# Half of q's norm on ScalarE, fused additions on GpSimd, later stores and loads: one change to a tuned attention + MLP kernel

## The chip, the cores and the metric

One core of one Trainium2 chip. The metric is the device time of one execution in microseconds (us). "Start" and "end" times inside a profile count from the start of its span. In this kernel TensorE does the matrix products (busy 1379.2 of 1399.7 us before the change) into PSUM, in banks that the program names; VectorE, ScalarE and GpSimd work beside it (busy 802.2, 419.6 and 581.7 us). The granted clock is the share of its full clock that the profile shows for TensorE.

## The reference, cut

```python
# q, k, v: (8, 12, 448, 64) f32;  w_in: (768, 2048), w_out: (2048, 768) f32
def rmsnorm(x, g):
    return x / np.sqrt(np.mean(x * x, axis=-1, keepdims=True) + 1e-06) * g
q_n, k_n = rmsnorm(q, g_q), rmsnorm(k, g_k)
attn = softmax(q_n @ k_n.T / sqrt(64))            # per batch and head
x = (attn @ v) -> (8*448, 12*64)                  # heads side by side
out = relu(x @ w_in) ** 2 @ w_out                 # (3584, 768)
```

The heads are handled two at a time: 48 pairs. The first twelve pairs (i = 0 to 11) run alone, and beside them GpSimd prepares the weights: each product of the MLP is done with seven block products instead of eight (Strassen's way), which needs sums of weight blocks (S1 to S4). The other pairs run beside the second product. The change touches the first twelve pairs, 0 to about 135 us, and the start of the first product after it.

## The kernel before: the parts concerned

```python
# weights: four ticks a tile t (generator; a tick after each part of an attention iteration)
    n = t - 3
    if there(n) and n % 2:                                  # tick 1: store of a finished pair of tiles, 1.3 MB
        nc.sync.dma_start(dst, blocks_of(n)[:, 0:7]); written[0] = n + 1
    nc.vector.tensor_scalar(e, e, ..., ALU.max, ALU.min)
    yield                                                   # tick 2: ScalarE and VectorE (cut)
    yield                                                   # tick 3
    nc.vector.scalar_tensor_tensor(eu, high, 0xC0000000, bits, ...)
    total(t - 2, S3, A11, A21, ALU.subtract)                # total: one GpSimd addition of 128x384
    total(t - 2, S4, A12, S2, ALU.subtract)
    value(t - 1, 0)                                         # value: one GpSimd addition of 128x384
    yield                                                   # tick 4
    value(t - 1, 1)
    total(t - 1, S1, A21, A22, ALU.add)
    total(t - 1, S2, S1, A11, ALU.subtract)
    load_words(t, t - 1); yield
...
def norm(i):                                                # (cut)
    nc.scalar.activation(sq, raw, AF.Square)
    nc.vector.tensor_reduce(rstd, sq..., AX, ALU.add)
    nc.vector.tensor_scalar(rstd, rstd, 1.0 / D, 1e-6, ALU.mult, ALU.add)
    nc.gpsimd.tensor_tensor(flat, flat, mhalf, ALU.pow)     # rstd ** -0.5
    nc.gpsimd.tensor_tensor(sq[:, 0]..., raw[:, 0]..., rstd..., ALU.mult)   # q's norm, 112x512
...
def add_up(i, c):                                           # the "running sum" of the softmax
    nc.vector.tensor_tensor(acc, probs[i, 0] if c == 1 else acc, probs[i, c], ALU.add)   # 112x896
...
for i in range(NAT):                                        # attention_alone, one iteration (cut)
    if 0 < i < NAT - 3:
        load(i + 3)                                         # q and k of pair i+3
    scores(i, 0); scores(i, 1)                              # matmuls, then exponentials on ScalarE
    transpose(i + 1, 1, 0)                                  # k, PSUM bank 0, then a copy by ScalarE
    values(i - 1, (2, 3)); add_up(i, 1); norm(i + 2)
    yield
    transpose(i + 1, 0, 0)                                  # q, PSUM bank 0 as well
    load_v(i + 1); yield
    scores(i, 2); scores(i, 3); total_of(i - 1); values(i, (0, 1)); finish(i - 1); yield
    if added(i) == 3: add_up(i, 2)                          # odd iterations
    combine_x(i - 1); yield
values(i, (2, 3)); total_of(i); finish(i); combine_x(i)     # the last pair
```

All loads and stores shown go through one queue, that of SyncE (SP), in program order: a store that waits for GpSimd holds up every load behind it (until 74.88 us in the third reading below).

Of the kernel before, what the change touches and what calls it, by code (L numbers as in the profile page):

```python
# [9 lines left out]
F32 = mybir.dt.float32  # L10
U32 = mybir.dt.uint32
AF = mybir.ActivationFunctionType
# [291 lines left out]
def places_of(qk, i, work):  # L304


    first, second = i % 2 * 4 + work, i % 2 * 4 + 2 + (i // 2 + work) % 2
    return qk[:, first:second + 1:second - first]
# [78 lines left out]
def attention_then_ffn_bounded(  # L387
# [100 lines left out]


    A11, S2, S1, S3, A12, A22, S4 = range(7)  # L490
    A21 = 7
    w1s = dram.tile([HF, 7, P, HW], F32, name="w1s")
    w2s = dram.tile([7, HF // 4, P, 4, HW], F32, name="w2s")

# [4 lines left out]
    def words_of(n):  # L499
        place = n % WORDS  # L500
        if place == 0:
            at = BLOCKS * 8 * HW + EXPS * NW
            flat = stage[:, at:at + 2 * NW]
        elif place < 3:
            f = (NFC, HF)[place - 1] - 2
            flat = gT[:, f:f + 2, :].rearrange("p f n -> p (f n)")[:, 0:2 * NW]
        else:
            if (n, "words") not in spare:
                spare[n, "words"] = spare["pool"].tile([P, 2 * NW], F32, tag="words", name="words", bufs=WORDS - 3)
            flat = spare[n, "words"]  # L510
        return flat.bitcast(U32)

    def blocks_of(n):
        at = n // 2 % BLOCKS * 8 * HW
        return stage[:, at:at + 8 * HW].rearrange("p (k m) -> p k m", k=8)
# [27 lines left out]
    def prepare(t):  # L543



        def there(n):
            return 0 <= n < 2 * NFC

        def parts(n):  # L550
            low, high = pairs_of(words_of(n))
            return exponents_of(n), exponents_of(n).bitcast(U32), low, high

        def value(n, half):
            if not there(n):
                return

            to = ((A11, A12), (A21, A22)) if n < NFC else ((A11, A21), (A12, A22))
            dst = blocks_of(n)[:, to[n % 2][half]]
            part = slice(half * HW, (half + 1) * HW)  # L560
            if doubles:
                _, eu, low, _ = parts(n)
                nc.gpsimd.tensor_tensor(*[x.bitcast(I32) for x in (dst, low[:, part], eu[:, part])], ALU.add)  # L563
            else:
                nc.gpsimd.tensor_copy(dst, words_of(n).bitcast(F32)[:, part])

        def total(n, dst, x, y, op):
            if there(n) and n % 2:
                nc.gpsimd.tensor_tensor(*[blocks_of(n)[:, i] for i in (dst, x, y)], op)  # L569

        def unsigned(n):

            if there(n) and doubles:
                e, _, _, high = parts(n)
                nc.scalar.activation(e, high.bitcast(F32), AF.Abs)

        if t == 0:
            unsigned(0)
        n = t - 3
        if there(n) and n % 2:  # L580
            c = n % NFC // 2
            dst = w1s[c] if n < NFC else w2s[:, c // 4, :, c % 4]
            nc.sync.dma_start(dst.rearrange("k p m -> p k m"), blocks_of(n)[:, 0:7])
            written[0] = n + 1
        if there(t) and doubles:
            e, eu, low, high = parts(t)

            nc.vector.tensor_scalar(e, e, 2.0 ** -15, 1.875 * 2.0 ** 16, ALU.max, ALU.min)
        yield
        if there(t) and doubles:  # L590
            nc.scalar.activation(low.bitcast(I32), low, AF.Copy, scale=2.0 ** -29)
            bits = banks.get("bits", eu)
            nc.vector.tensor_scalar(bits, eu, 3, 0x3FFFFFF8, ALU.logical_shift_left, ALU.bitwise_and)
        if t < 3:
            load_words(t, t - 1)
        yield
        if there(t) and doubles:
            nc.vector.scalar_tensor_tensor(eu, high, 0xC0000000, bits, ALU.bitwise_and, ALU.bitwise_or)
        total(t - 2, S3, A11, A21, ALU.subtract)
        total(t - 2, S4, A12, S2, ALU.subtract)  # L600
        value(t - 1, 0)
        yield
        unsigned(t + 1)
        value(t - 1, 1)
        total(t - 1, S1, A21, A22, ALU.add)
        total(t - 1, S2, S1, A11, ALU.subtract)
        load_words(t, t - 1)
        yield

# [45 lines left out]
    def load(i):  # L655
        if i < NAT:
            load_q(nc, qk, q, i)
            load_k(nc, qk, k, i)
            return

        b, h0 = i // NPAIR, 2 * (i % NPAIR)
        for s, src in enumerate((q, k)):
            dst = by_squares(i, 0)[:, s]
            for n in range(4):
                nc.sync.dma_start(dst[n * 32:(n + 1) * 32],
                                  src[b, h0 + n // 2, :, n % 2 * 32:n % 2 * 32 + 32]
                                  .rearrange("(g t) e -> t g e", t=32))
# [16 lines left out]
    def norm(i):  # L684
        if i >= NAT:
            squares(i)
            return norm_by_squares(i)
        raw, sq = (places_of(qk, i, n)[:SP] for n in range(2))
        rstd = rstds[i] = small.tile([SP, 2, 2 * NJ], F32, tag="rstd", name="rstd", bufs=4)
        normed[i] = sq[:, 0], raw[:, 1]  # L690
        if i <= 2:
            return normalise_in_turn(nc, raw, sq, rstd, mhalf)
        nc.scalar.activation(sq, raw, AF.Square)
        nc.vector.tensor_reduce(rstd, sq.rearrange("p s (n d) -> p s n d", d=D), AX, ALU.add)
        nc.vector.tensor_scalar(rstd, rstd, 1.0 / D, 1e-6, ALU.mult, ALU.add)
        flat = rstd.rearrange("p s n -> p (s n)")
        nc.gpsimd.tensor_tensor(flat, flat, mhalf[:SP, 0:4 * NJ], ALU.pow)  # L697

        nc.gpsimd.tensor_tensor(sq[:, 0].rearrange("p (j h d) -> p h j d", j=NJ, h=2),  # L699
                                raw[:, 0].rearrange("p (h j d) -> p h j d", j=NJ, h=2),  # L700
                                rstd[:, 0].rearrange("p (h j) -> p h j ()", h=2).to_broadcast([SP, 2, NJ, D]),
                                ALU.mult)

    def squares(i):
        raw, qkn = (by_squares(i, n).rearrange("p s g e -> p (s g e)") for n in range(2))
# [27 lines left out]
    def transpose(i, s, n):  # L733

        pt = bank("pt", n)
        for j in range(NJ):
            nc.tensor.transpose(pt[:, j * SP:(j + 1) * SP], normed[i][s][:, j * P:(j + 1) * P], ident[:SP, :SP])  # L737
        if s:
            nc.scalar.copy(qkT[:, i % 2, s], pt)
        else:  # L740
            nc.scalar.activation(qkT[:, i % 2, s], pt, AF.Copy, scale=gains[:, 0:1])
# [58 lines left out]
    def values(i, chunks=range(NJ)):  # L800
        if 0 in chunks:
            pavs[i] = ps_o.tile([P, S], F32, tag="o", name="pav") if i >= NAT or i % 2 == 0 else bank("pav", 1)
        for c in chunks:
            for h in range(2):
                nc.tensor.matmul(pavs[i][h * D:(h + 1) * D, :], vs[i][:, h, c, :], probs[i, c][:, h, :],  # L805
                                 start=(c == 0), stop=(c == NJ - 1))
# [49 lines left out]
    def attention_alone():  # L856


        for i in range(NAT):
            more = i + 1 < NAT  # L860
            if 0 < i < NAT - 3:
                load(i + 3)
            scores(i, 0)
            scores(i, 1)
            if i == 0:

                transpose(1, 1, 1)
                scores(0, 2)
                scores(0, 3)
                transpose(1, 0, 0)  # L870
                add_up(0, 1)
                norm(2)
                load_v(1)
                values(0, (0, 1))
                load(3)
                yield
                continue
            if more:
                transpose(i + 1, 1, 0)
            values(i - 1, (2, 3))  # L880
            add_up(i, 1)
            if i + 2 < NAT:
                norm(i + 2)
            elif not more:
                norm(NAT)
                load(NAT + 2)
            yield
            if more:
                transpose(i + 1, 0, 0)
            load_v(i + 1)  # L890
            yield
            scores(i, 2)
            scores(i, 3)
            total_of(i - 1)
            values(i, (0, 1))
            finish(i - 1)
            yield
            if added(i) == 3:
                add_up(i, 2)
            combine_x(i - 1)  # L900
            if NAT <= i + 3 < NAT + 2:
                load(i + 3)
            yield
        values(i, (2, 3))
        total_of(i)
        finish(i)
        combine_x(i)

# [321 lines left out]
```

## Time and profile before

| | before |
|---|---|
| device time | 1400.38 us (3 runs, 1400.37 to 1401.83) |
| TensorE busy | 1379.2 of 1399.7 us |
| GpSimd / VectorE busy, 20 to 140 us | 106.2 / 105.1 of 120 us |
| first product starts | 134.21 us |

The prediction below shows the page and TensorE's waits. Groups of instructions further below, 20 to 140 us, are given as line, engine, operation, output and input, count, then busy us and mean ns of one, then the idle time before them with what ended it.

The timeline of VectorE and of GpSimd (start, length, engine, line, operation):

```profile
71.07 1.96 DVE L764 TENSOR_TENSOR gT<-gT 112x896 f32<-112x896 f32 x1
72.95 1.21 DVE L694 TENSOR_REDUCE rstd<-qk 112x16 f32<-112x1024 f32 x1
```

### The profile page before, as it was taken

The page shows a single profiled execution, that of the slowest core. Times are in us where ns is not written, and L with a number is a line of the kernel's source. Part 1 is how long each engine was busy: PE and PEld are TensorE (multiplying, and loading weights), DVE is VectorE, ACT ScalarE, POOL GpSimd, SP SyncE. Part 2 cuts the span into 40 slices and gives each one's busy share as a digit, 9 for nine tenths or more (in the row PEclk, how much of TensorE's full clock was granted, in tenths as well). Part 3 has the DMA queues.
Part 4 walks back from the last instruction along what each step waited for, and adds up shares of the span by engine and source line. Part 5 has one row for each costly group of instructions (what it writes and reads, how often), then busy time and mean ns, then how long its engine had stood idle before and what let it go on. Part 6 is the DMA issues. An engine that isn't in the chain of part 4 may idle for free.

```text
span 1399.7 us, 14445 instructions
## 1 busy us (share of the span) xinstructions
PE 1379.2 (99%) x4450; PEld 638.5 (46%) x4450; DVE 802.2 (57%) x1398; ACT 419.6 (30%) x621; POOL 581.7 (42%) x400
## 2 busy tenths in 40 slices
PE   8989999999999999999999999999999999999997
PEld 3333455444444454544444455444444445554553
DVE  6889676589876234476777523457777633332111
ACT  7875556432322011233332011233333201110000
POOL 5998877444552123544453122544445302221000
PEclk9999999999999999999999999999999999999999
DMA  9687998545764332344665333344564332334443
GB/s 240 189 229 199 341 384 306 143 97 120 144 121 105 102 90 85 104 113 110 127 130 119 97 94 90 98 106 105 129 126 102 95 101 85 90 87 104 106 111 70
DMA packets 430915, 188.79 MB, mean 135 GB/s; under 512 B 277484, under 2 KB 428780, under 8 KB 430828
## 3 DMA queue, kind: packets, MB, share of 16 engines
q1 hardware_dynamic: 421228, 179.05, 49.8%
q10 hardware_dynamic: 9472, 8.72, 2.3%
q8 instruction: 38, 0.62, 0.2%
q14 instruction: 49, 0.40, 0.1%
q0 software_dynamic: 128, 0.00, 0.0%
HBM read 154.54 MB, written 33.16 MB: 134 GB/s over the span
## 4 chain that ended last, share of the span: by engine, by line
PE 93%; POOL 3%; DVE 1%; DMA 1%; ACT 1%; issue 1%; ACTq 0%; POOLq 0%
PE ps L1047 37%; PE sc L749 10%; PE pd L1000 10%; PE pa L1000 10%; PE pc L1000 10%; PE pav L805 9%; PE pb L1000 5%; PE tot L819 1%; POOL rstd L697 1%; POOL gC L563 1%; DMA sw<-w1s 1%; POOL gC L569 1%; PE pt L737 0%; ACT gT L754 0%; POOL qk L699 0%
## 5 line engine op out<-in xcount | busy, mean ns | idle before, releaser
L1047 PE MATMUL ps<-gT,sw 128*128 128x448 f32 x768 | 299.2, 543 | 0.8 <-POOL gT L977 0.8
L719 POOL TENSOR_TENSOR half<-half,mhalf 128x28 f32<-128x28 f32 x36 | 173.6, 4822 | 266.9 <-DVE half L718 226.8
L1047 PE MATMUL ps<-gC,sw 128*128 128x448 f32 x576 | 225.2, 543 | 0.0
L977 POOL TENSOR_TENSOR gT<-gT 128x448 f32<-128x448 f32 x96 | 94.9, 990 | 309.9 <-ACT gT L973 309.9
L1047 PEld LDWEIGHTS ps<-gT,sw 128*128 128x128 f32 x768 | 144.1, 190 | 150.7 <-issue 147.0
L756 ACT ACTIVATE pr<-sc 112x896 f32<-112x896 f32 x120 | 104.7, 914 | 293.4 <-PE sc L749 184.9
L749 PE MATMUL sc<-qkT 64*112 64x448 f32 x768 | 170.6, 563 | 0.9 <-ACT qkT L383 0.8
L1047 PEld LDWEIGHTS ps<-gC,sw 128*128 128x128 f32 x576 | 108.2, 190 | 112.1 <-issue 110.8
L1000 PE MATMUL pa<-xT,sw 128*128 128x448 f32 x384 | 154.9, 540 | 0.0
L973 ACT ACTIVATE gT<-gT 128x448 f32<-128x448 f32 x96 | 55.3, 577 | 310.1 <-DVE gT L1015 310.0
L749 PEld LDWEIGHTS sc<-qkT 64*112 64x112 f32 x768 | 61.2, 173 | 97.9 <-issue 81.3
L1000 PEld LDWEIGHTS pa<-xT,sw 128*128 128x128 f32 x384 | 73.0, 190 | 71.6 <-issue 70.3
L805 PE MATMUL pav<-pr,vt 112*64 112x448 f32 x480 | 100.2, 547 | 0.0
L721 POOL TENSOR_TENSOR qk<-qk,half 128x448 f32<-128x448 f32 x72 | 81.3, 1150 | 2.8
L764 DVE TENSOR_TENSOR acc<-acc,pr 112x896 f32<-112x896 f32 x60 | 68.2, 1136 | 21.0 <-ACT pr L756 18.5
L1000 PE MATMUL pb<-xC,sw 128*128 128x448 f32 x192 | 77.6, 540 | 1.5 <-issue 1.5
L1000 PE MATMUL pd<-xT,sw 128*128 128x448 f32 x192 | 77.9, 542 | 0.0
L1000 PE MATMUL pc<-xC,sw 128*128 128x448 f32 x192 | 77.5, 540 | 0.2 <-DMA sw<-w1s 0.2
L1000 PE MATMUL pd<-xC,sw 128*128 128x448 f32 x192 | 77.5, 540 | 0.0
L1000 PE MATMUL pc<-xT,sw 128*128 128x448 f32 x192 | 77.4, 539 | 0.0
L1015 DVE TENSOR_TENSOR gT<-z,pd 128x448 f32<-128x448 f32 x32 | 19.8, 620 | 99.7 <-PE pd L1000 99.7
L569 POOL TENSOR_TENSOR gC<-gC 128x384 f32<-128x384 f32 x64 | 72.8, 1157 | 2.5
(120 smaller groups left out, 1551.0 us busy)
## 6 DMA issues: line engine op xcount, KB each, us to landing
sw<-w1s SPq DMA_DIRECT2D x224, 192.0 KB, 2.3
sw<-w2s SPq DMA_DIRECT2D x168, 256.0 KB, 3.3
w1s<-gC SPq DMA_DIRECT2D x8, 1344.0 KB, 7.5
w2s<-gC SPq DMA_DIRECT2D x8, 1344.0 KB, 7.6
out_dram<-osb SPq DMA_DIRECT2D x184, 56.0 KB, 1.9
qk<-in_q_dram SPq DMA_DIRECT2D x144, 56.0 KB, 3.0
qk<-in_k_dram SPq DMA_DIRECT2D x144, 56.0 KB, 2.9
vt<-in_v_dram SPq DMA_DIRECT2D x72, 112.0 KB, 2.9
```

Source lines behind the costliest of these rows:

```text
L569: nc.gpsimd.tensor_tensor(*[blocks_of(n)[:, i] for i in (dst, x, y)], op)
L719: nc.gpsimd.tensor_tensor(half, half, mhalf, ALU.pow)
L721: nc.gpsimd.tensor_tensor(qkn[:, s], raw[:, s], half[:, s * NG:(s + 1) * NG].rearrange("p g -> p g ()").to_broadcast([P, NG, 32]), ALU.mult)
L749: nc.tensor.matmul(sc[:, h, 0:S], qkT[rows, at, 1, c * SP:(c + 1) * SP], qkT[rows, at, 0, :], start=True, stop=True)
L756: nc.scalar.activation(pr, sc[:, :, 0:S], AF.Exp)
L764: nc.vector.tensor_tensor(acc, probs[i, 0] if c == 1 else acc, probs[i, c], ALU.add)
L805: nc.tensor.matmul(pavs[i][h * D:(h + 1) * D, :], vs[i][:, h, c, :], probs[i, c][:, h, :], start=(c == 0), stop=(c == NJ - 1))
L973: nc.scalar.activation(g, src, AF.Relu)
L977: nc.gpsimd.tensor_tensor(g, g, g, ALU.mult)
L1000: nc.tensor.matmul(ps, stream[n + i][:, c], rhs[:, c], start=first and c == 0, stop=c == HC - 1, skip_group_check=not first)
L1015: add(g, x, ps, ALU.add)
L1047: nc.tensor.matmul(ps, stream[n][:, c % 4], rhs_of[i][:, c], start=c == 0, stop=c == HF - 1)
```

## The change

Its intent is to take work from GpSimd, which limits the stage at 80 to 100 us (busy 19.5 of 20 us, TensorE 16.3): four small ScalarE operations do the first head of q's norm an iteration later, and additions on neighbouring blocks become one operation of 768 elements. ScalarE now reads q's buffer later, so the load of pair i+3 moves to the end of the iteration; the weight store moves two ticks down. Odd iterations use the other PSUM bank for q's transpose, and the end is reordered.

```diff
-    A21 = 7
+    A21 = -1
...  (store: from tick 1 to tick 3)
-        total(t - 2, S3, A11, A21, ALU.subtract)
-        total(t - 2, S4, A12, S2, ALU.subtract)
-        value(t - 1, 0)
+        total(t - 2, (S3, S4), (A11, A12), (A21, S2), ALU.subtract)     # one operation of 768
         yield
+        value(t - 1)                                                    # one operation of 768
         unsigned(t + 1)
-        value(t - 1, 1)
-        total(t - 1, S1, A21, A22, ALU.add)
-        total(t - 1, S2, S1, A11, ALU.subtract)
+        total(t - 1, (S1,), (A21,), (A22,), ALU.add)
+        total(t - 1, (S2,), (S1,), (A11,), ALU.subtract)
...  (norm: GpSimd multiplies only the second head, 112x256)
+    def norm_q(i):
+        if 2 < i < NAT:
+            dst, src, factors = q_of(i, 0)
+            for j in range(NJ):
+                nc.scalar.activation(dst[:, j], src[:, j], AF.Copy, scale=factors[:, j:j + 1])
...
-            if 0 < i < NAT - 3:
-                load(i + 3)
             scores(i, 0)
             scores(i, 1)
...
+            norm_q(i + 1)
             if more:
                 transpose(i + 1, 1, 0)
...
-                transpose(i + 1, 0, 0)
+                transpose(i + 1, 0, i % 2)
...
             finish(i - 1)
+            if i + 3 < NAT:
+                load(i + 3)
             yield
...
-        values(i, (2, 3))
+        values(i, (2,))
         total_of(i)
+        values(i, (3,))
```

More of the change, by code (lines that the diff above doesn't have):

```diff
@@ L552, in parts, with put, blocks, value @@
             return exponents_of(n), exponents_of(n).bitcast(U32), low, high
-        def value(n, half):
+        def put(op, *places):
+            lone = any(len(x) == 2 and x[1] <= x[0] for _, x in places)
+            for take in [slice(0, 1), slice(1, 2)] if lone else [slice(0, 2)]:
+                op(*[of[:, x[take][0]:x[take][-1] + 1:max(x[take][-1] - x[take][0], 1)] for of, x in places])
+        def blocks(n, *which):
+            return blocks_of(n), [1 + i for i in which]
+        def value(n):
             if not there(n):
@@ L558, in value, with add @@
             to = ((A11, A12), (A21, A22)) if n < NFC else ((A11, A21), (A12, A22))
-            dst = blocks_of(n)[:, to[n % 2][half]]
-            part = slice(half * HW, (half + 1) * HW)
+            halves = [x.rearrange("p (two m) -> p two m", two=2) for x in
+                      ((parts(n)[2], parts(n)[1]) if doubles else (words_of(n),))]
             if doubles:
-                _, eu, low, _ = parts(n)
-                nc.gpsimd.tensor_tensor(*[x.bitcast(I32) for x in (dst, low[:, part], eu[:, part])], ALU.add)
-            else:
-                nc.gpsimd.tensor_copy(dst, words_of(n).bitcast(F32)[:, part])
+                def add(*x):
+                    nc.gpsimd.tensor_tensor(*[y.bitcast(I32) for y in x], ALU.add)
+            else:
+                def add(dst, src):
+                    nc.gpsimd.tensor_copy(dst, src.bitcast(F32))
+            put(add, blocks(n, *to[n % 2]), *[(x, [0, 1]) for x in halves])
         def total(n, dst, x, y, op):
             if there(n) and n % 2:
-                nc.gpsimd.tensor_tensor(*[blocks_of(n)[:, i] for i in (dst, x, y)], op)
+                put(lambda *z: nc.gpsimd.tensor_tensor(*z, op), *[blocks(n, *i) for i in (dst, x, y)])
         def unsigned(n):
@@ L578, in prepare @@
             unsigned(0)
-        n = t - 3
-        if there(n) and n % 2:
-            c = n % NFC // 2
-            dst = w1s[c] if n < NFC else w2s[:, c // 4, :, c % 4]
-            nc.sync.dma_start(dst.rearrange("k p m -> p k m"), blocks_of(n)[:, 0:7])
-            written[0] = n + 1
         if there(t) and doubles:
@@ L596, in prepare @@
         yield
+        n = t - 3
+        if there(n) and n % 2:
+            c = n % NFC // 2
+            dst = w1s[c] if n < NFC else w2s[:, c // 4, :, c % 4]
+            nc.sync.dma_start(dst.rearrange("k p m -> p k m"), blocks_of(n)[:, 1:8])
+            written[0] = n + 1
         if there(t) and doubles:
             nc.vector.scalar_tensor_tensor(eu, high, 0xC0000000, bits, ALU.bitwise_and, ALU.bitwise_or)
-        total(t - 2, S3, A11, A21, ALU.subtract)
-        total(t - 2, S4, A12, S2, ALU.subtract)
-        value(t - 1, 0)
+        total(t - 2, (S3, S4), (A11, A12), (A21, S2), ALU.subtract)
         yield
+        value(t - 1)
         unsigned(t + 1)
-        value(t - 1, 1)
-        total(t - 1, S1, A21, A22, ALU.add)
-        total(t - 1, S2, S1, A11, ALU.subtract)
+        total(t - 1, (S1,), (A21,), (A22,), ALU.add)
+        total(t - 1, (S2,), (S1,), (A11,), ALU.subtract)
         load_words(t, t - 1)
@@ L697, in norm, with q_of @@
         nc.gpsimd.tensor_tensor(flat, flat, mhalf[:SP, 0:4 * NJ], ALU.pow)
-        nc.gpsimd.tensor_tensor(sq[:, 0].rearrange("p (j h d) -> p h j d", j=NJ, h=2),
-                                raw[:, 0].rearrange("p (h j d) -> p h j d", j=NJ, h=2),
-                                rstd[:, 0].rearrange("p (h j) -> p h j ()", h=2).to_broadcast([SP, 2, NJ, D]),
-                                ALU.mult)
+        dst, src, factors = q_of(i, 1)
+        nc.gpsimd.tensor_tensor(dst, src, factors.rearrange("p j -> p j ()").to_broadcast([SP, NJ, D]), ALU.mult)
+    def q_of(i, h):
+        raw, sq = (places_of(qk, i, n)[:SP, 0] for n in range(2))
+        return (sq.rearrange("p (j h d) -> p h j d", j=NJ, h=2)[:, h],
+                raw.rearrange("p (h j d) -> p h j d", j=NJ, h=2)[:, h], rstds[i][:, 0, h * NJ:(h + 1) * NJ])
+    def norm_q(i):
[3 more added lines that the diff above has]
+                nc.scalar.activation(dst[:, j], src[:, j], AF.Copy, scale=factors[:, j:j + 1])
     def squares(i):
```

## The prediction

> **What bounds the kernel now.** I read the page first: busy shares, then the chain that ended last.
>
> ```profile
> PE 1379.2 (99%) x4450; PEld 638.5 (46%) x4450; DVE 802.2 (57%) x1398; ACT 419.6 (30%) x621; POOL 581.7 (42%) x400
> PE 93%; POOL 3%; DVE 1%; DMA 1%; ACT 1%; issue 1%; ACTq 0%; POOLq 0%
> ```
>
> TensorE is busy 1379.2 of 1399.7 us. The order of TensorE's work hardly changes (the instruction order shows the same groups, only the last block sum moves ahead of the last two value products), so no more than the 20.5 us of TensorE idling can be won, and 2% of 1400 us is 28 us. What matters is where the 20.5 us lie. The table of stretches of 20 us answers that for the stage that the change touches (attention of the first twelve pairs, with the preparation of the weights beside it, 0 to about 135 us, then the first product until 260 us); its columns are the length and each engine's busy time with its count:
>
> ```profile
> core 0: us, PE busy (x) PEld busy (x) DVE busy (x) ACT busy (x) POOL busy (x), PEclk, DMA share, GB/s
> 20.00:40.00 20.00, 18.64 (x88) 7.02 (x88) 17.02 (x26) 14.86 (x25) 12.56 (x8) 0.91 0.93 250
> 40.00:60.00 20.00, 20.00 (x108) 7.99 (x108) 17.87 (x23) 17.18 (x30) 19.04 (x12) 1.00 0.60 173
> ...
> 80.00:100.00 20.00, 16.30 (x86) 6.24 (x84) 16.02 (x20) 14.10 (x24) 19.53 (x15) 1.00 1.11 299
> ...
> 120.00:140.00 20.00, 17.73 (x79) 6.56 (x76) 19.36 (x30) 6.62 (x12) 15.57 (x11) 1.00 0.73 195
> 140.00:160.00 20.00, 19.81 (x52) 9.46 (x51) 14.22 (x18) 10.53 (x16) 17.00 (x16) 1.00 0.98 327
> ```
>
> From 140 to 400 us TensorE lacks 0.2 us, so work saved there wins nothing. At 40 to 60 us TensorE is the bound; at 80 to 100 us it falls to 16.3 while GpSimd stands at 19.5: GpSimd has become the bound. TensorE's own waits up to 250 us name the losses (total, times, longest):
>
> ```profile
> PE pt L737 <- POOL qk L699: 4.4, 4, 2.3
> PE pt L737 <- ACT qkT L739: 1.9, 1, 1.9
> PE pb L1000 <- issue: 1.5, 1, 1.5
> PE tot L819 <- DVE gT L832: 0.8, 1, 0.8
> ```
>
> Only the first three or four can be reached: 8.6 us, 0.6%. The timeline shows the mechanism. GpSimd's power operation starts once a pair: 44.91, 56.09, 67.34, 78.14, 90.55, 100.69, 110.53 us, 65.62/6 = 10.94 us a pair. TensorE alone needs 9.26 us in an even iteration and 10.02 in an odd one (starts of the score matmuls at 29.13, 38.39, 48.40, 57.67 us), 9.64 on average. GpSimd falls behind 1.3 us a pair, uses up its lead of some 3 us, and from about 70 us the transposes of q wait for it.
>
> [...] 128x448 by a gain pointer 655 ns [...], the plain copy 554 [...], four exponentials back to back in 2.21 us. [...] Here 384 elements take 987 ns at least and 448 take 1127: 2.19 ns an element, 0.15 us fixed. [...] the same 384-element operation takes 987 to 2324 ns. [...] The trace grants 0.91 in 20 to 40 us, right after the 1.9 us wait at 19.4 us.
>
> **The change, part by part.**
> 1. Half of q's norm leaves GpSimd. L699 multiplies 512 elements in 1.04 us (lowest; mean 1.29). A 448-element product takes 0.93 us, so about 1.65 ns an element and 0.2 us fixed; 256 elements are some 0.62 us. Saved: 0.42 us a pair, perhaps 0.6 as loaded.
> 2. Fusing. Two additions of 384 become one of 768, and S3 with S4 likewise. Elements stay, the fixed 0.15 to 0.18 us goes. Per weight tile that is one saving, and half of one for S3/S4; 1.17 tiles a pair: 0.30 us a pair. Together GpSimd goes from 10.9 to about 10.0 us a pair. [...]
> 3. ScalarE gets four ACTIVATEs of 112x64 with a pointer scale a pair: [...] 0.95 us a pair [...]. ScalarE is busy 17.2 of 20 us at 40 to 60 us, 8.3 us a pair; it becomes about 9.2 of 9.6 to 10. It fits, but not freely.
> 4. Where the four stand matters more. In ScalarE's order they come after the first four exponentials and before the copy of k's transpose. In an even iteration q's transpose uses the same PSUM bank as k's and must wait for that copy. In iteration 4 the score matmuls start at 48.40, the copy ends at 52.17, q's transpose starts at 52.31: no wait, but no room. With 0.95 us more the copy ends at about 53.1: TensorE waits some 0.85 us. Odd iterations now use the other bank (the new i % 2) and wait only for the last of the four pieces, about 0.05 us. Iterations 2, 4, 6, 8, 10: 5 x 0.85 = 4.25 us of new waiting, 4 x 0.05 = 0.2 more.
> 5. What it removes: iterations 2 to 10 of before last from 29.13 to 120.47 us, 91.34 us; TensorE's own work is 5 x 9.26 + 4 x 10.02 = 86.4. So 5.0 us were lost. After: TensorE with its new waits needs 10.1 us a pair, GpSimd 10.0, so GpSimd no longer falls behind. 5.0 - 4.45: a gain of only about 0.5 us.
> 6. Iteration 1 gains by the other bank: there q's transpose waited from 19.37 to 21.36 us for the copy of k's. Now it waits for the norm of q on VectorE, which ends at 19.26, so about 1.9 us go; the scores behind it wait for exponentials and give back 0.4: 1.5 us. The half-clock stretch after it cost about 1.7 us (3.4 us at half), and may go too[...], and the timed runs (1400.37, 1400.38, 1401.83) look as if most had been spared it; I count 0.4.
> 7. Stores and loads later. The load of pair i+3 has to wait now for ScalarE's half, and comes a half to three quarters of an iteration later. In the steady state it lands about 3 us after issue, with some 3 us left. At the start the queues are full (DMA share 0.93 to 1.17 at 15 to 30 us; pair 4's q took 9.6 us to land), and pair 4 now stands behind 1 MB more, about 3 us: its square may hold ScalarE up around 33 us and eat part of point 6. I take 0.3 off.
> 8. The end. TensorE's 0.8 + 1.5 us there are VectorE's: it is busy without a break from 119.08 to 138.1 us. The reordered block sum moves the wait, not VectorE's work: 0 to 0.5 us.
>
> Sum: 0.5 + 1.5 + 0.4 - 0.3 + 0.4 = 2.5 us: **1397.9 us**.
>
> **The rivals.**
> A. ScalarE's four operations cost nothing on TensorE (the wait of point 4 is hidden, or falls where TensorE would wait anyway). Then the full 4.4 us of waits for GpSimd vanish, with iteration 1's: 6 to 7 us, about 1394. For it: the even iterations that waited longest for GpSimd (6 and 8) can swap one wait for the other. Against it: iterations 2 and 4 had no wait at all, and the copy ended only 0.14 us before the transpose.
> B. GpSimd stays behind: the additions are bound by elements, not by instructions[...]. At 10.5 us a pair the waits at the end of the stage remain on top of those for ScalarE, or, as ScalarE itself now waits in order for the power operation, its exponentials stand still too. Then 1400 to 1402. For it: 4.67 additions a pair took 6.3 us where unloaded they take 4.7, and fusing removes only 0.3.
> C. Late loads take over: the square of a pair waits for DMA as once before (1.97 us for k at 83.22 us). The DMA share of 0.6 to 1.1 and the 1.3 MB stores in the same queue speak for it. 1 to 3 us worse.
> D. Nothing moves: TensorE's work is the time and waits only change their name, 1400 +- 0.7.
>
> **Range and chances.** B or C costs at most 4 us from my sum, A gives at most 4. So 1395.0 to 1400.8 holds it 8 times in 10. Neither side reaches 28 us: within 2% with 0.985.
>
> **What would show it.** GpSimd: the interval of power operations about 10 us, its norm about 0.6 us, fused additions about 1.83 us unloaded. [...] TensorE: the wait for L699 near zero, a new wait of q's transpose for ScalarE, some 0.8 us in even iterations alone; the wait at 19.4 us gone; the first product starting 2 to 3 us earlier, and the same length of everything after it. I am wrong if the even waits are missing (rival A), if q's transposes still wait for GpSimd after 80 us (B), if squares wait for DMA (C), or if the time changes after 140 us.

Of the single operations timed there, those of 128x448 and the exponentials are ScalarE's, those of 384 and 448 elements GpSimd's additions. The 0.95 us of point 3 was my estimate; the kernel before has no such operation. Its trace gives some 0.85 us, again as an estimate: squares of 512 and 1024 elements took 630 and 1096 ns, so 0.91 ns an element; the copy of 448 with a pointer scale took 658, so one of 64 is some 0.31 us; and four in a row overlap by 0.13 us each if they do as the four exponentials of 0.65 us did, in 2.21 us.

## More of the kernel before

```profile
70.33 1.75 POOL L699 TENSOR_TENSOR qk<-qk,rstd 112x512 f32<-112x512 f32 x1
72.04 2.81 POOL L569 TENSOR_TENSOR gC<-gC 128x384 f32<-128x384 f32 x2
```

The sum arrives at 71.07 while GpSimd multiplies until 72.08. It takes 1.96 us instead of its 1.08 alone: it stands still for the rest of that one GpSimd instruction and then runs, before GpSimd's next two, which take 2.81 us instead of twice 0.99. Both lose a little, once.

The timeline of the SP queue (a line is a DMA issue). The store waits for GpSimd until 74.88, and the pair's q and k come directly behind it:

```profile
74.88 0.38 SPq L583 DMA_DIRECT2D w1s<-gC  x1
75.35 0.51 SPq L315 DMA_DIRECT2D qk<-in_q_dram  x1
75.99 2.53 SPq L325 DMA_DIRECT2D qk<-in_k_dram  x2
78.56 0.69 SPq L532 DMA_DIRECT2D words<-in_moe_w_in_dram  x1
79.79 0.92 SPq L678 DMA_DIRECT2D vt<-in_v_dram  x1
```

The running sum, and the power operation that starts GpSimd's part of the norm:

```profile
L764 DVE TENSOR_TENSOR gT<-gT 112x896 f32<-112x896 f32 x16 | 20.9, 1312 | 3.2 <-ACT gT L754 3.2
...
L697 POOL TENSOR_TENSOR rstd<-rstd,mhalf 112x16 f32<-112x16 f32 x9 | 28.4, 3155 | 7.8 <-PE sc L749 4.6 <-DVE rstd L695 3.1
```

## The result, and the profile after

| | before | after |
|---|---|---|
| device time, same chip and rounds | 1401.11 us (4 runs, 1400.37 to 1403.38) | 1410.74 us (4 runs, 1409.77 to 1410.98) |
| first product starts | 134.21 us | 139.56 us |
| from there to the last matmul's end | 1258.4 us | 1262.2 us |
| VectorE busy, 20 to 140 us | 105.1 us | 116.1 us |
| GpSimd busy, 20 to 140 us | 106.2 us | 92.9 us |

The ratio is 1.0065, 95% interval 1.0047 to 1.0082. A ratio here is the mean time of one kernel's fast runs over that of the other's of the same rounds, as recorded; the listed times give it when the profiled execution of each is left out, so it is not quite the ratio of the medians. Within 2%, but slower by some 9 us, outside the range. Below, "+9.1 us" for a ratio of 1.0065 means 0.0065 x 1402 us. The ratios' intervals are about 0.0017 wide on each side, 2.4 us, so a difference between two ratios is uncertain by some 3.4 us.

TensorE's waits after (total, times, longest):

```profile
PE pt L758 <- ACT qkT L760: 5.2, 4, 2.7
PE pt L758 <- POOL qk L711: 3.0, 3, 1.5
PE pd L1023 <- DMA sw<-w1s: 2.7, 1, 2.7
PE tot L840 <- DVE gT L853: 2.1, 1, 2.1
```

The waits for GpSimd did not vanish, those for ScalarE came on top as foreseen, and there is a wait for weights that was 0.2 us before. The groups that answer to those of before:

```profile
L785 DVE TENSOR_TENSOR gT<-gT 112x896 f32<-112x896 f32 x16 | 35.7, 2236 | 0.0
...
L708 POOL TENSOR_TENSOR rstd<-rstd,mhalf 112x16 f32<-112x16 f32 x9 | 30.4, 3375 | 18.2 <-DVE rstd L706 13.6 <-PE pav L826 4.4
```

The running sum, which the change does not touch, takes 2236 ns instead of 1312. VectorE has hardly a gap left, and GpSimd, which should have been the winner, now idles 13.6 us for VectorE's reductions. The timelines of the two engines at the place that answers to the one shown of before:

```profile
72.32 5.12 DVE L785 TENSOR_TENSOR gT<-gT 112x896 f32<-112x896 f32 x1
77.37 1.21 DVE L705 TENSOR_REDUCE rstd<-qk 112x16 f32<-112x1024 f32 x1
```

```profile
70.69 2.21 POOL L711 TENSOR_TENSOR qk<-qk,rstd 112x256 f32<-112x256 f32 x1
72.86 1.82 POOL L581 TENSOR_TENSOR gC<-gC 128x768 f32<-128x768 f32 x1
74.64 1.85 POOL L573 TENSOR_TENSOR gC<-words,gC 128x768 int32<-128x768 int32 x1
78.86 3.42 POOL L708 TENSOR_TENSOR rstd<-rstd,mhalf 112x16 f32<-112x16 f32 x1 [2.37 <-DVE rstd L706]
```

The sum arrives at 72.32, 0.6 us before L711 ends, and does not run then: it ends at 77.44, its own 1.0 us after the third GpSimd instruction in a row. Its delay goes to the reduction (77.37), from there to the next power operation (78.86, which waited 2.37 us), ScalarE and TensorE. I call this the conflict of the two engines; the traces show whom it hits and for how long, not what makes it. It does not hit every VectorE operation: in 20 to 140 us the reduction took 1.20 to 1.23 us throughout, the sum 1.08 to 5.12. Nor does every GpSimd instruction block the sum for its whole length. In before, two sums ran undisturbed inside one power operation:

```profile
91.32 1.10 DVE L764 TENSOR_TENSOR gT<-gT 112x896 f32<-112x896 f32 x1
92.88 1.08 DVE L764 TENSOR_TENSOR gT<-gT 112x896 f32<-112x896 f32 x1
...
90.55 3.62 POOL L697 TENSOR_TENSOR rstd<-rstd,mhalf 112x16 f32<-112x16 f32 x1
```

The instructions that the sum was seen to wait for are the norm's product and the additions (L699 at 71 us in before; L711, L581 and L573 at 72 to 76 us in after).

The SP queue after, at the same place, and at the start of the first product:

```profile
74.71 0.39 SPq L608 DMA_DIRECT2D w1s<-gC  x1
75.15 0.55 SPq L532 DMA_DIRECT2D words<-in_moe_w_in_dram  x1
75.81 1.30 SPq L689 DMA_DIRECT2D vt<-in_v_dram  x1
77.22 1.27 SPq L315 DMA_DIRECT2D qk<-in_q_dram  x1
79.02 1.39 SPq L325 DMA_DIRECT2D qk<-in_k_dram  x2
...
145.51 0.48 SPq L608 DMA_DIRECT2D w1s<-gC  x1
146.03 0.56 SPq L535 DMA_DIRECT2D gT<-in_moe_w_out_dram  x1
146.69 2.43 SPq L693 DMA_DIRECT2D vt<-in_v_dram  x2
149.22 2.58 SPq L657 DMA_DIRECT2D sw<-w1s  x4
```

At 75 us the pair's q and k are now the last behind the store, not the first. At 145 us a store of 1.3 MB stands before the weights (sw) that TensorE waits for 2.7 us at 152.7; before, that store was issued at 123.44, and those sw loads at 142.49. The granted clock in 140 to 160 us fell to 0.91 (0.50 from 155.9 to 159.2 us). It is also below 1 at 80 to 120 us (0.95 and 0.97; 0.50 from 97.8 to 101.2), behind the 2.7 us wait for ScalarE, and at 0 to 20 us (0.91; 0.50 from 9.1 to 12.4, in iteration 0, which the change leaves alone); in before it is below 1 at 20 to 40 us only (0.91; 0.50 from 22.3 to 25.7, behind a wait of 1.9 us). Each stretch at 0.50 lasts 3.4 us and comes after TensorE has idled. But behind a wait of 2.25 us in before (until 95.34), and behind one of 1.9 us for ScalarE in e16, the clock stayed at 1.00: these traces give no rule. Part of the loss thus comes by way of the clock, in stretches behind waits; how much was not separated.

Two suspects follow, the conflict (theory P: the sum stands still behind GpSimd's instructions, longer behind longer ones) and the order of the queue, and one cost foreseen, the even waits for ScalarE. The experiments have to divide 9 us among them.

### The profile page after: what moved, and what is told of

Read it like the earlier page. It is cut to its first block, busy times and chain, and to the rows that moved or that the text cites. A ratio compares the mean times of both kernels' runs of the same rounds, so it can differ in the third digit from the quotient of the medians.

```text
span 1408.8 us, 14399 instructions
## 1 busy us (share of the span) xinstructions
PE 1383.2 (98%) x4450; PEld 639.0 (45%) x4450; DVE 819.4 (58%) x1398; ACT 428.4 (30%) x657; POOL 567.8 (40%) x360
## 4 chain that ended last, share of the span: by engine, by line
PE 93%; POOL 1%; issue 1%; ACT 1%; DMA 1%; DVE 1%; SPq 1%; POOLq 0%; ACTq 0%
PE ps L1070 36%; PE sc L770 11%; PE pd L1023 10%; PE pc L1023 10%; PE pa L1023 10%; PE pav L826 9%; PE pb L1023 5%; PE tot L840 1%; PE pt L758 1%; DMA qk<-in_k_dram 1%; POOL rstd L708 0%; ACT gT L775 0%; DMA sw<-w1s 0%; DVE gT L785 0%; POOL gC L581 0%
## 5 line engine op out<-in xcount | busy, mean ns | idle before, releaser
L581 POOL TENSOR_TENSOR gC<-gC 128x384 f32<-128x384 f32 (+1 forms) x48 | 71.7, 1495 | 3.5
```

Source lines behind the costliest of these rows:

```text
L581: put(lambda *z: nc.gpsimd.tensor_tensor(*z, op), *[blocks(n, *i) for i in (dst, x, y)])
```

## The experiments

Each text says what its letters stand for. Ratios are to the kernel before, run on the same chip in the same rounds; each diff is against the kernel named first.

### Undoing and isolating the fusing

**e1**: the changed kernel, every fused addition split again into two of 384.

```diff
-            for take in [slice(0, 1), slice(1, 2)] if lone else [slice(0, 2)]:
+            for take in [slice(n, n + 1) for n in range(max(len(x) for _, x in places))]:
```

> The changed kernel with only the fusing undone: every GpSimd addition of the weights is again two of 384 elements, at the same place in the order. Theory P [...]: VectorE's running sum of 112x896 falls from a mean of 2236 ns to about 1300 ns as in the kernel before, VectorE's busy time in 20 to 140 us from 116 to about 105 us, GpSimd's waits for VectorE's rstd go, and the time falls to 1398 to 1402 us. Rival N (the half norm on ScalarE and the late loads cause the loss): the sum stays above 2000 ns or the time stays within 2 us of 1410. Rival S (late stores): the wait of the first product for its weights, 2.7 us, and the half clock after it stay, time 1405 to 1408.

Measured: 1412.18 us, 1.0066; running sum 1903 ns, VectorE 113.0 us. Unfusing cures nothing. So the fused length is not the only thing that stops the sum.

**e2**: the kernel before with only the fused additions (and their layout, A21 = -1, and the first half a tick later); nothing else of the change.

> The kernel before with only the fusing (and with it the place of the first half's addition, one tick later); norm, loads, stores and banks as before. Theory P: the running sum of 112x896 rises to 1900 ns or more and the time to 1405 to 1410 us. Rival N: the running sum stays near 1300 ns and the time within 1.5 us of 1400.4, or falls.

Measured: 1409.24 us, 1.0057; running sum 2167 ns, VectorE 116.1 us. Fusing by itself costs 8 us (0.0057 x 1402) although it leaves GpSimd less to do.

**e5**: the kernel before with only the placement of e2: both halves in tick 4, unfused.

```diff
-        value(t - 1, 0)
         yield
+        value(t - 1, 0)
+        value(t - 1, 1)
         unsigned(t + 1)
-        value(t - 1, 1)
```

> The kernel before with one thing of the change: the addition of a weight tile's first half moves a tick later, beside the second half's, still as two operations of 384 elements; norm, loads, stores, banks and the layout of the blocks as before. Theory R (what hurts is that GpSimd's operations now stand in one unbroken run, whatever their length, and VectorE's running sum stands still until the run ends): mean of the running sum from 1.31 to about 1.8 to 2.2 us, VectorE busy over 113 us in 20 to 140 us, time 1406 to 1410. Theory F (what hurts is the length of a fused operation, 1.83 us instead of two of 0.99): running sum stays at 1.3 us, VectorE about 105, time 1400 to 1402.

Measured: 1401.99 us, 0.9995; running sum 1324 ns. The placement is innocent: it is the operation's length (or the new layout, which came with it). My theory of the unbroken run "whatever its length" is wrong in that form.

**e6**: the changed kernel with the weight preparation of before (unfused, two ticks, old layout); the norm, banks, end and late queue of after stay.

> The changed kernel with the weight preparation of before (no fusing, the two halves in two ticks, old layout), but with ScalarE's part of the norm, late loads and stores, the other bank and the reordered end. Theory R: GpSimd's operations are spread as before, so the running sum falls back to 1.3 to 1.5 us unless the short norm (0.6 us) itself lets no one in; time 1397 to 1401. Theory N (a GpSimd operation with less than about 0.6 us left when VectorE arrives keeps VectorE out until the whole run ends, so the short norm is itself harmful): running sum 1.7 us or more, time 1404 or more.

Measured: 1411.92 us, 1.0061; running sum 2103 ns. Without any fusing the sum is blocked as well. Here VectorE arrives during the short norm of 0.6 us.

### Does the blocked sum set the time?

**e8**: the changed kernel with a one-column copy on GpSimd after the norm and after each addition, which reads what was just written and so makes a pause in the run: in the timeline below the copy begins 0.06 us after the operation it reads has ended, while the two additions in the timeline of after each begin 0.04 us before the one ahead has ended.

```diff
+    def gap(x):
+        nc.gpsimd.tensor_copy(scrap[:x.shape[0]], x)
```

> The changed kernel with a tiny copy (one column) on GpSimd after the norm and after each addition; each reads the result just written, so GpSimd must wait for its own operation to end, which puts a pause into the run. Theory R (unbroken runs keep VectorE out): running sum back to 1.2 to 1.5 us, VectorE under 107 us in 20 to 140 us, time 1397 to 1402, although GpSimd executes more. Rival F (VectorE is blocked by the fused operations' length alone): running sum stays at 1.8 us or more and the time at 1409 or more. If VectorE's arrivals depend on something else (its own late start), neither moves much.

Measured: 1411.66 us, 1.0066; running sum 1413 ns, VectorE 103.3 us, GpSimd 104.3 us. Half of the theory holds: a pause lets VectorE in, and its sum is back to almost what it was. But the time did not move. GpSimd's timeline in this run shows one reason:

```profile
72.34 2.21 POOL L716 TENSOR_TENSOR qk<-qk,rstd 112x256 f32<-112x256 f32 x1
74.61 0.93 POOL L527 COPY scrap<-qk 112x1 f32<-112x1 f32 x1
75.50 1.81 POOL L586 TENSOR_TENSOR gC<-gC 128x768 f32<-128x768 f32 x1
```

The copy of one column, 0.18 us where nothing is in its way, takes 0.93 us: now GpSimd stands still for the sum (73.97 to 75.49 us, 1.52 us here). In these timelines the conflict takes its time from the one or from the other. And ScalarE's squares waited 6.8 us for k's DMA between 60 and 112 us, so the queue has a part too.

**e10** and **e11**: the sum's second input taken away, in the changed kernel and in the one before. The result is wrong; the engine, order and elements are the same.

```diff
+        if i < NAT:
+            return nc.vector.tensor_reduce(acc, probs[i, c].rearrange("p h q -> p h q ()"), AX, ALU.add)
         nc.vector.tensor_tensor(acc, probs[i, 0] if c == 1 else acc, probs[i, c], ALU.add)
```

> The changed kernel with a wrong result on purpose: VectorE's running sum (two SBUF inputs) replaced, in the first twelve pairs, by a reduction over an axis of length one of the same 112x896 elements (one SBUF input; the other reduction in the traces is never stretched by GpSimd). Same engine, same order, same waits but for the second input. Theory P [...]: these operations take 1.0 to 1.1 us each throughout, VectorE under 103 us in 20 to 140 us, power operations about 10 us apart, and the time falls to what I predicted, 1396 to 1400. Theory L (late loads, queue order): VectorE recovers but the square still waits for k and the time stays at 1406 or more.

> The kernel before with the same replacement (wrong result on purpose), as the control of the run above[...]. Theory P: GpSimd gains 1.57 us a pair (its additions no longer wait for the sum), power operations 9.6 to 10.2 us apart instead of 10.9, TensorE's 4.4 us of waits for GpSimd mostly gone: 1396 to 1399. Theory L: little change, 1400 to 1402.

Measured: e10 1404.31 us, 1.0013, between the two ranges expected; e11 1398.46 us, 0.9968, as theory P expected. The replaced sums took 1082 and 1075 ns on average, undisturbed. So the sum's part in the conflict, with what follows from it, is worth 0.0065 - 0.0013 = 0.0052, 7.3 us (give or take 3.4), in the changed kernel, and 0.0032, 4.5 us, in the one before. TensorE's two largest waits in e10:

```profile
PE pt L758 <- ACT qkT L760: 5.2, 5, 1.8
PE pd L1025 <- DMA sw<-w1s: 3.0, 1, 3.0
```

The waits for GpSimd are gone, as predicted for the change; the even waits for ScalarE and the wait for weights are left. But without the sum's part in the conflict on either side the change still costs 0.0045, 6.3 us. The part of the conflict that the change added, 7.3 - 4.5 = 2.8 us, is not the main one: my theory P fails as the whole explanation.

### The order of the queue

**e3**: the changed kernel with the store back at its old place (tick 1); the loads late. **e4**: the same on top of e1.

> The changed kernel with the stores of the weight tiles at their old place, two ticks earlier; all else as changed. Rival S: the first product's wait for its weights (2.7 us) and the half clock after it (1.8 us) go: 1405 to 1407 us. Theory P: the attention stage is untouched, the start of the first product stays 5 us late, and the wait for weights shrinks only partly because the loads in front of it in the queue still wait for GpSimd: 1406 to 1410 us.

> The changed kernel with fusing undone and stores at their old place: what is left is q's half norm on ScalarE, the other bank in odd iterations, the later loads and the block sum at the end. Theory P and the prediction's sum without the 0.3 us a pair of fusing: 1397 to 1401 us. Rival N: above 1404 us.

Measured: e3 1414.1 us, 1.0094, above both ranges expected; e4 1415.4 us, 1.009, as rival N had it. The wait for weights is gone in both, and a worse one has come. TensorE's longest wait in e3:

```profile
PE sc L770 <- ACT gT L775: 9.6, 3, 8.1
```

and ScalarE's:

```profile
ACT qk L704 <- DMA qk<-in_k_dram: 11.6, 2, 10.7
```

The load of pair 8, which the changed kernel issued at 62.33 us, now stands behind a store that waits for GpSimd until 74.83; ScalarE's square waits 10.7 us for it, and the exponentials behind the square free no PSUM for the scores, for which TensorE waits 8.1 us. Moving the loads without the stores would have been worse still than the change.

**e9**: the changed kernel with the loads sooner, right after ScalarE's four operations; the store late.

```diff
             norm_q(i + 1)
+            if i + 3 < NAT:
+                load(i + 3)
```

> The changed kernel with the loads of q and k of pair i+3 issued right after ScalarE's four operations, half an iteration sooner than in the change. Theory L (late loads: ScalarE's square waits 4.0 us for k from 60 to 112 us, and passes it on to VectorE's reduction, GpSimd's power operation and TensorE): the square's wait falls under 1.5 us, TensorE's 2.7 us wait at 94.6 us shrinks to under 1 us, time 1404 to 1407. Theory P [...]: the running sum stays at 1.9 to 2.3 us, power operations still over 11 us apart on average between 57 and 103 us, time 1408 to 1412.

Measured: 1408.41 us, 1.004. The square's waits for DMA are gone from the list of ScalarE's waits; TensorE still waits 3.8 us for weights and up to 3.6 us for GpSimd. The gain is 0.0025, about 3.5 us, hardly more than its uncertainty. The wait of theory L went, but the time stayed above its 1404 to 1407 us.

**e14**: both, so that stores and loads are issued in the order of before.

> The changed kernel with stores and loads back in the order of before (the store at its old place, the pair's loads right after ScalarE's four operations). If the wait for weights (2.7 us after 152 us, and the half clock behind it) comes from the moved store: it is gone, everything from the first product's start to the end takes 1257 to 1259 us instead of 1262, time 1403.5 to 1406. If the queue order has no part in it: the wait stays, 1408 to 1411. The running sum stays at 1.8 us or more.

Measured: 1404.15 us, 1.001. The four corners, as ratios to before:

| | store late (as changed) | store at its old place |
|---|---|---|
| loads late (as changed) | 1.0065 (after) | 1.0094 (e3) |
| loads sooner | 1.0040 (e9) | 1.0010 (e14) |

The order of the queue is worth 0.0065 - 0.0010 = 0.0055, 7.7 us (give or take 3.4), the largest part of the loss, and putting back either half alone does not bring it. (With the sum out of the conflict, e10 against e15 below, the same step is worth 0.0013 + 0.0024 = 0.0037, 5.2 us: the two causes are not independent.) In e14's trace the first product starts at 137.16 instead of 139.56 us, and from there to the end it takes 1258.0 us instead of 1262.2, as in the kernel before: 2.4 + 4.2 = 6.6 us in the two traces. The stretch of 140 to 160 us (columns: PE, PEld, DVE, ACT, POOL busy with counts, granted clock, DMA share, GB/s), first after, then e14:

```profile
140.00:160.00 20.00, 16.39 (x38) 7.41 (x37) 12.87 (x16) 4.26 (x7) 16.53 (x12) 0.91 0.84 259
```

```profile
140.00:160.00 20.00, 19.65 (x51) 9.59 (x52) 14.06 (x17) 9.42 (x16) 16.90 (x10) 1.00 0.95 293
```

The weights' wait and the lost clock are gone from this stretch; TensorE gets 3.3 us more done there. In the attention stage e14's trace has lost more clock than after's (0.87 and 0.96 at 80 to 120 us, against 0.95 and 0.97), behind a wait of 3.6 us for GpSimd: what is left of the change's loss lies there.

### What is left without queue and conflict

**e15**: e14 with the one-input sum of e10 (wrong). **e16**: e2, the fusing alone, with the one-input sum (wrong).

> The run above with the running sum replaced by the one-input reduction (wrong result on purpose)[...]. What is left against the kernel before with the same replacement (1398.5) is ScalarE's even waits minus iteration 1's gain, which I put at 4.45 - 1.5 = 3 us less the 1.8 us of waits for GpSimd left there: 1399 to 1401.5. If a further cost of the change is unknown to me, it stays at 1402 or more.

> The kernel before with only the fused additions (e2, 1409.2) and the one-input reduction in place of the running sum (wrong result on purpose). If the harm of fusing goes entirely through VectorE's sum standing still behind GpSimd: 1397 to 1400, as the kernel before with that replacement (1398.5). If fused additions cost something else (later results for the stores, ScalarE held up): 1403 or more.

Measured: e15 1399.71 us, 0.9976; e16 1401.08 us, 0.9988. In e15 what is left of the change against e11, the control, is 0.0008, 1 us: within the intervals nothing. Its only waits above 2 us in sum are those for ScalarE, 5.7 us in five, which fits the foreseen even waits eating what the unloading of GpSimd gives. The sum's part in the conflict costs 0.0034 in e14, 4.8 us, against 4.5 us in before: once the queue is in order, the conflict costs no more than it did, although the sum still takes 2035 ns there. In the changed queue's order it cost 7.3. I read this as slack that the late loads had used up, but the difference of 2.5 us is no larger than the intervals, so it is not shown.

With the fusing alone, taking the sum out of the conflict (e2 to e16) brings the ratio from 1.0057 to 0.9988: 9.7 us, where the same step in the kernel before brings 4.5. So about 5 of the 8 us that fusing costs go through the sum, and e16 falls between the two ranges expected. Against e11 some 2.8 us (0.9988 - 0.9968) remain, and the groups of e16 show another VectorE operation in the sum's place. VectorE's clipping of the weights, first in e11, then in e16:

```profile
L588 DVE TENSOR_SCALAR gC<-gC 128x768 f32<-128x768 f32 x13 | 9.9, 758 | 0.0
```

```profile
L600 DVE TENSOR_SCALAR gC<-gC 128x768 f32<-128x768 f32 x13 | 16.6, 1277 | 0.0
```

It takes 0.55 us undisturbed (74.80 us in before). So when the sum is taken out of the way of the long additions, the clipping takes longer, as if it stood still behind them in the sum's place. That the rest of e16 is due to this is likely, not shown.

**e18**: the kernel before with the norm's half on ScalarE, the other bank and the new end; additions, stores and loads as before.

> ScalarE's half of the norm, the other bank and the reordered end, with stores and loads in the order of before and the additions of before (nothing fused, old layout, halves in two ticks). If the norm's loss in e6 (1411.9) came from the queue order: 1400 to 1404. If the short norm on GpSimd harms by itself[...]: 1406 or more, running sum over 1.9 us.

Measured: 1406.24 us (5 runs), 1.0036, interval 1.0022 to 1.0049; running sum 2106 ns. Neither expectation is met: it lies between. The short norm is enough to get the sum blocked, with no fused addition in the kernel. Fusing alone cost 8 us, this part alone 5, both with the queue in order (e14) only 1.4. The costs do not add up. That would fit either part being enough to make VectorE wait, while both together leave GpSimd less to do; I did not separate the two.

### Towards a faster version

**e7**: the kernel before with the other bank only. **e19**: with the other bank and the new end. **e12** and **e17**: e7 with 11 or 12 instead of 13 weight tiles prepared beside the attention.

```diff
-                transpose(i + 1, 0, 0)
+                transpose(i + 1, 0, i % 2)
...  (e12; e17 has 12)
-    EARLY, ALL = 4 * 13, 4 * (2 * NFC + 3)
+    EARLY, ALL = 4 * 11, 4 * (2 * NFC + 3)
```

> The kernel before with only the other PSUM bank for q's transpose in odd iterations. My prediction's point 6: the 1.9 us wait of iteration 1 goes, some 1.5 us of it stay won: 1399 to 1400, running sum unchanged at 1.3 us. If instead the time gained early is eaten by GpSimd being the bound of the stage (its power operations every 10.9 us), the time does not move: 1401 as before.

> The kernel before with [...] the other bank in odd iterations and the last block sum ahead of the last two value products. The bank alone measured 0.9992 of before; the end loses the 0.8 us wait for VectorE or the 1.5 us after it. I expect 1398.5 to 1400.5, a ratio of 0.998 to 0.999, so faster than both kernels, though by little; if GpSimd's pace decides the stage it is 1401 to 1402, no gain.

> A candidate to beat both: the kernel before with the other bank in odd iterations and 11 instead of 13 weight tiles prepared beside the attention; the other two follow in the first product, where TensorE waits for nothing on GpSimd. Theory P [...]: 2 tiles are some 8 additions or 8 us of GpSimd less in 90 us, power operations about 10 us apart, TensorE's waits for GpSimd under 2 us, time 1394 to 1398. If the loads of k are the bound instead: 1398 to 1401. If the first product now waits for weights: over 1401.

> Candidate to beat both: as e12 but 12 instead of 11 tiles beside the attention. With 11 the first product started 4.6 us sooner and lost 3.0 us to waits for weights and DMA afterwards. With 12: starts 2 to 4 us sooner, loses 1 or less: 1397.5 to 1400. If the loss afterwards comes with any tile moved: 1401 to 1402.

Measured: e7 1400.97 us, 0.9992 (0.9975 to 1.0009); e19 1401.42 us, 0.9998 (0.9984 to 1.0011); e12 1402.0 us, 1.0002; e17 1402.09 us, 0.9998. None is faster than before. In e7's trace the second iteration's scores start at 25.9 instead of 29.1 us, and the first product only at 133.0 instead of 134.2: the 3.2 us won early shrink to 1.2, and TensorE's waits for GpSimd grow from 4.4 to 6.0 us, which fits GpSimd's pace setting the stage's end. In e19's trace nothing is won early: with the same bank, TensorE waits 1.8 us for the exponentials instead, and the second iteration's scores start at 29.27. In e12 the first product starts 4.6 us sooner, at 129.62 us, and the time from there to the end grows by 3.0 us to 1261.5, with waits for weights there; its timed runs show no gain at all. No version here with a right result beats both.

## Why the prediction was wrong, point by point

- **Point 7 (late loads and stores, -0.3 us) is the step that failed most.** It was mis-sized: the four corners give it 7.7 us. I looked at how long a load takes to land in the steady state, and not at the order of the one queue: a store that waits for GpSimd releases everything behind it at once (from 74.71 us on in after), and the pair's loads had gone from first to last in that burst. And I followed the moved store only to 140 us: at 145.51 it stands before the first product's weights, 2.7 us of waiting and a stretch of 3.4 us at a granted clock of 0.50. Rival C named the right mechanism with 1 to 3 us. "The same length of everything after" the first product's start was wrong for this reason: 1262.2 instead of 1258.4 us.
- **Points 2 and 5 (GpSimd at 10.0 us a pair, its waits gone) failed.** The operations' own lengths were right: 1.82 to 1.85 us for a fused addition, 0.61 for the norm. But power operations came at 44.9 and six pairs later at 114.0 us, 11.5 us a pair, more than the 10.9 of before. I had counted GpSimd's busy time as its own, and had read the 987 to 2324 ns of one and the same addition only as GpSimd's loss. The change made VectorE the loser: the sum went from 1312 to 2236 ns. In e14, with the queue in order, TensorE still waits 6.5 us for GpSimd where I had the 4.4 us of before vanish; e14's +1.4 us is 4.2 above my own sum without point 7 (-2.8), close to those 4.4, which may be chance. Rival B saw that GpSimd would stay behind, not that VectorE would pay.
- **Points 1 and 3 were right**: 0.61 us for GpSimd's half (0.62 foreseen), 1.07 us for ScalarE's four (0.95).
- **Point 4 was right where GpSimd was not later**: q's transpose waited 0.89, 0.82 and 0.83 us in iterations 2, 4 and 10 (0.85 foreseen). In iterations 6 and 8 longer waits took its place: 1.27 us for GpSimd, and 2.71 us for ScalarE, which had itself waited 1.44 us for the power operation (95.72), as the second half of rival B had it.
- **Point 6 was right for this trace and worth little**: the 1.9 us wait went, and the second iteration started 2.2 us sooner. e7 shows that most of it is given back by the end of the stage, and e19 that the gain can fail to come. The stretch at a granted clock of 0.50 did not go: it lay at 22.3 to 25.7 us in before and lies at 9.1 to 12.4 in after.
- **Point 8**: the wait of the last block sum for VectorE grew from 0.8 to 2.1 us and the one behind it fell from 1.5 to 0.7: no gain; e19 shows none either.

Open: why VectorE gets in after one GpSimd instruction in the kernel before and only after three in the changed one. Every long stall that I looked at in the changed kernel and in e6 began during the short norm with less than 0.6 us left of it; in e2 also with up to 1.0 us left, so that is no rule.

## What to carry to other kernels

Before moving a load or a store, write down the order of its whole queue, with what each entry waits for, to the end of the stage and past it: here the order cost 7.7 us, and putting back either half alone left most of it or added to it. Where two engines hold each other up, as here, a profile's busy time holds the waiting (5.12 us for a sum of 1.08 and 116.1 busy us of 120 on VectorE, 0.93 us for a copy of 0.18 on GpSimd), so count both engines' undisturbed work together: unloading or regrouping the one may only choose who pays. A control in which the suspected conflict did not occur (sums of 1082 and 1075 ns), run in both kernels, shows what it is worth; here it showed that the first suspect was the smaller part.
